# Queries and keys in two float32r parts over 48 rows, with two heads' scores as a pair of row tiles

## The chip, the cores and the metric

The kernel runs on one core of a Trainium2 chip. A core has a matmul engine (TensorE, PE in the profile; its weight loads are listed apart as PEld), VectorE (DVE), ScalarE (ACT), GpSimd (POOL), and queues that issue transfers (SP is the one most used here). They run side by side and wait for each other through semaphores. TensorE writes to eight banks of PSUM, 512 float32 columns each. The metric is the device time of one execution in microseconds, given as the median of several runs. A profile is one further execution with every instruction recorded.

## What is computed

Two rounds of two layers on a residual stream of 2048 tokens by 512. The first layer is full attention with 32 query heads of 16 columns and one common key and value head; the second works in four segments of 512 tokens, with a key and value head for each query head, a mask, and a memory that the segments before have written.

```python
def _A_ref(x, wq, wk, wv, wo):                 # full attention
    q = heads((x @ wq)); k = x @ wk; v = x @ wv
    p = softmax(q @ k.T * 0.25)
    return merge(p @ v) @ wo

def _B_ref(x, wq, wk, wv, wo, beta):           # segment attention with memory
    for s in range(4):
        p = softmax(qs @ ks.T * 0.25 + mask)
        a_mem = (phi(qs) @ M) / (phi(qs) @ z + 1e-6)
        outs.append(g * a_mem + (1 - g) * (p @ vs))
        M += phi(ks).T @ vs;  z += phi(ks).sum()
    return merge(outs) @ wo

x = A_x
x = x + _A_ref(layernorm(x), ...);  x = x + _B_ref(layernorm(x), ...)
x = x + _A_ref(layernorm(x), ...);  x = x + _B_ref(layernorm(x), ...)
```

(Shortened; the names are the reference's, `heads` and `merge` stand for its reshapes.) All of it is float32.

## The kernel before

**Blocks and streams.** Tokens go in four blocks of 512. While the full attention of one block of queries runs (`a_units`), everything that follows from the block before is computed beside it (`side`: output projection, layer norm, segment attention `b_block`, second output projection, and in the first round the inputs of the next full attention, `a_prep`). `weave` (L306) orders the two streams on TensorE while the program is built: it keeps an account of when each engine gets done (`pe`, `on`), and gives the next turn to the stream that lags in proportion to its length. The order is fixed at build time; on the chip TensorE takes its instructions in that order and waits where an operand is late. `finish` (L323) completes a block's full attention alone once the other stream is through.

**Exact products of queries and keys.** A projection's result is split by `split3` (L422) into three bfloat16 parts: one copy on GpSimd (L120) and three operations on VectorE (L428 to L430). The parts go through a scratch in DRAM (`sd`), from which `a_load` and `b_load` lay six groups of 16 rows into the tiles `qa`, `qb` and `kb`; the keys of the full attention are laid out on chip by L444 to L446 into `kst`. Each head's score is one matmul over 96 rows of contraction, and one or two more rows subtract the softmax guard.

**Full attention, a stage.** One stage is one tile of 128 keys for four heads and 512 queries. L600 computes the scores of two heads into two PSUM banks, ScalarE takes the exponential of both at once (L603, 1024 columns), and this is done twice. The products with the values (`a_pv`, L625) are plain float32: four heads go to four column tiles of 17 columns of the array at once. They appear at L77 (the first of a group) and L80 (the other three), since `together` (L74) issues them; a plain float32 matmul shows as two records. There are 1024 stages.

**Segment attention.** `b_inputs` (L710) projects and splits queries and keys and computes their feature maps; `b_rowmax` (L759) computes all scores once for the row maxima, L771, which VectorE takes at L779; `guard_rows` (L546) puts the maxima into rows 96 and 97 of the queries; `b_attend` (L791) computes the scores again with these rows, transposed (L807), adds the mask by a further matmul of 128 columns (L810), and goes on with the exponential (L814) and the values (`b_pv`). Columns that the mask leaves out whole are not computed, so the matmuls have 512, 384, 256 or 128 columns.

**Projections.** `project` (L332) multiplies operands in two float32r parts, three matmuls for each of four contraction tiles (L341), 128 rows and 512 columns each.

## Time and profile before

| | us |
|---|---|
| median of 3 runs | 3379.58 |
| lowest, highest | 3378.01, 3379.90 |
| span of the profiled execution | 3373.7 |
| TensorE busy in it | 3289.8 |
| ScalarE busy in it | 2404.7 |
| VectorE busy in it | 1644.6 |

The span runs from the first to the last instruction; the time of a run holds a little more. Busy time counts an engine as busy from an instruction's start to its end. Matmuls follow each other in a pipeline, so that the length of one is longer than the distance to the next: the distance between starts tells what one costs.

In the lists of costly groups a row names line, engine, operation, tiles and shapes, then the count; behind the first bar the busy time and the mean length of one in ns; behind the second the engine's idle time ahead of them and what ended it. A row of the timeline has start and length in us, then engine, line, operation, tiles, shapes and how many instructions it merges. A row by stretch has start and end, length, busy time of the engines with counts in brackets, the granted TensorE clock, the share of the transfer engines and what they moved in GB/s.

### The profile page before, as it was taken

Reading aid. Unit: us, or ns where it says so; the run is one execution under the profiler, and the core shown is the slowest. Engines: PE = TensorE matmul, PEld = TensorE weight load, DVE = VectorE, ACT = ScalarE, POOL = GpSimd, SP = SyncE. Lnnn points to the kernel's source line nnn. Section 1 sums busy time; section 2 is a strip of 40 time slices with the busy share of each in tenths; the row PEclk is TensorE's granted clock in tenths of the full one; section 3 lists DMA queues with packets and bytes.
Section 4 is the critical chain, followed back from the end, with each engine's and each line's share of the span. In section 5 each row is a group of like instructions: output and inputs, shape, how many; then the busy total and the mean of one; then the engine's idle time right before and its main releaser. Section 6 shows DMA issues by size and latency. Waiting matters only on the chain.

```text
span 3373.7 us, 53649 instructions
## 1 busy us (share of the span) xinstructions
PE 3289.8 (98%) x20586; PEld 1252.0 (37%) x20586; DVE 1644.6 (49%) x4679; ACT 2404.7 (71%) x2575; POOL 377.6 (11%) x540
## 2 busy tenths in 40 slices
PE   7999999999999999999999999999999999999977
PEld 4422333334333443334433333333433334333533
DVE  7701345454553545645455353555455534553466
ACT  3699777866778667786678878677677776778422
POOL 2100110021100220102110020100110002100100
PEclk9999999999999999999999999999999999999978
DMA  4411121122210231202322142321231215221341
GB/s 133 130 33 29 56 84 56 33 78 85 69 54 20 72 91 56 72 15 82 101 64 75 45 123 78 111 61 52 79 85 50 58 39 161 90 65 29 124 121 42
DMA packets 188674, 244.62 MB, mean 73 GB/s; under 512 B 26904, under 2 KB 147576, under 8 KB 188408
## 3 DMA queue, kind: packets, MB, share of 16 engines
q1 hardware_dynamic: 169272, 176.08, 17.7%
q0 software_dynamic: 19136, 65.02, 6.8%
q8 instruction: 164, 2.69, 0.4%
q14 instruction: 102, 0.84, 0.1%
HBM read 168.41 MB, written 72.61 MB: 71 GB/s over the span
## 4 chain that ended last, share of the span: by engine, by line
PE 80%; issue 8%; DVE 5%; DMA 4%; POOL 2%; ACT 1%; SPq 0%; DVEq 0%; POOLq 0%; ACTq 0%
PE bank L77 28%; PE bank L600 24%; PE bank L341 13%; PE bank L771 4%; PE bank L807 4%; PE bank L810 1%; PE bank L80 1%; DMA sb<-parts 1%; PE bank L832 1%; DVE mo L779 1%; DMA wst<-in_B_wq_dram 1%; PE bank L401 1%; POOL w L120 1%; PE bank L868 1%; ACT pa L603 1%
## 5 line engine op out<-in xcount | busy, mean ns | idle before, releaser
L603 ACT ACTIVATE pa<-bank 128x1024 f32<-128x1024 f32 x2048 | 2010.1, 1022 | 610.9 <-PE bank L600 597.2
L600 PE MATMUL bank<-qa,kst 97*128 97x512 bf16 x4096 | 1147.4, 381 | 3.1 <-ACT pa L603 1.8
L80 PE MATMUL bank<-pa,va 128*17 128x512 f32 x6144 | 1072.0, 598 | 0.0
L77 PE MATMUL bank<-pa,va 128*17 128x512 f32 x2048 | 1057.5, 598 | 2.9 <-DVE t L632 1.9
L779 DVE CUSTOM_DVE_ANT_0 mo<-bank,maskq 128x512 bf16<-128x512 f32 (+3 forms) x1024 | 498.7, 487 | 572.7 <-PE bank L771 557.8
L600 PEld LDWEIGHTS <-kst 97*128 97x128 bf16 x4096 | 313.8, 97 | 796.2 <-issue 640.0
L814 ACT ACTIVATE pb<-bank 128x1024 f32<-128x1024 f32 (+2 forms) x384 | 331.6, 881 | 179.8 <-PE bank L810 143.1
L341 PE MATMUL bank<-xh,w 128*128 128x512 f32 x832 | 322.1, 432 | 6.1 <-DVE qmx L471 2.7
L771 PE MATMUL bank<-kb,qb 96*128 96x512 bf16 (+3 forms) x1024 | 251.7, 309 | 26.4 <-DVE m L779 22.9
L341 PE MATMUL bank<-w,xh 128*128 128x512 f32 x752 | 269.8, 437 | 4.7 <-DVE xh L665 2.1
L77 PEld LDWEIGHTS bank<-pa,va 128*17 128x17 f32 x2048 | 117.5, 95 | 406.8 <-issue 325.2
L120 POOL TENSOR_SCALAR w<-wst 128x512 fp32r<-128x512 f32 x160 | 103.8, 649 | 1272.6 <-PE bank L341 1202.0
L807 PE MATMUL bank<-qb,kb 98*128 98x512 bf16 (+3 forms) x1024 | 222.9, 305 | 4.1 <-ACT pb L814 2.8
L632 DVE STREAM_TRANSPOSE t<-bank 128x512 f32<-128x512 f32 x88 | 62.8, 714 | 298.3 <-PE bank L80 297.9
L771 PEld LDWEIGHTS <-qb 96*128 96x128 bf16 x1024 | 87.2, 99 | 302.4 <-issue 247.2
L341 PEld LDWEIGHTS bank<-xh,w 128*128 128x128 f32 x832 | 158.4, 191 | 86.5 <-issue 32.7
L80 PE MATMUL bank<-pb,vb 128*17 128x512 f32 (+3 forms) x1536 | 186.0, 439 | 0.0
L77 PE MATMUL bank<-pb,vb 128*17 128x512 f32 (+3 forms) x512 | 182.6, 439 | 1.0 <-ACT pb L814 0.4
L341 PEld LDWEIGHTS bank<-w,xh 128*128 128x128 f32 x752 | 135.0, 189 | 109.5 <-issue 45.1
L341 PE MATMUL bank<-xl,w 128*128 128x512 f32 x416 | 166.5, 400 | 1.2 <-DVE xl L409 1.2
L208 DVE TENSOR_TENSOR w<-wst,w 128x512 fp32r<-128x512 f32 x160 | 112.0, 700 | 101.0 <-POOL w L120 100.2
L341 PE MATMUL bank<-w,xl 128*128 128x512 f32 x376 | 150.7, 402 | 0.0
(136 smaller groups left out, 2480.5 us busy)
## 6 DMA issues: line engine op xcount, KB each, us to landing
sb<-parts SPq DMA_DIRECT2D x192, 128.0 KB
qa<-sd SPq DMA_DIRECT2D x88, 196.0 KB
sd<-parts SPq DMA_DIRECT2D x96, 128.0 KB
x<-xt SPq DMA_DIRECT2D x48, 256.0 KB
xt<-x SPq DMA_DIRECT2D x48, 256.0 KB
qb<-sb SPq DMA_DIRECT2D x64, 192.0 KB
kb<-sb SPq DMA_DIRECT2D x64, 192.0 KB
qa<-sd SPq DMA_DIRECT2D x88, 128.0 KB
```

Source lines behind the costliest of these rows:

```text
L77: nc.tensor.matmul(*a, **k)
L80: tc.keep_in_program_order(nc.tensor.matmul(*a, **k))
L120: G.tensor_scalar(o, i, 1.0, 0.0, op0=ALU.mult, op1=ALU.add)
L208: V.tensor_tensor(w[:, 1, :], s, f(w[:, 0, :]), op=ALU.subtract)
L341: T.matmul(ps, lhsT=l_(kt), rhs=r_(kt), start=n == 0, stop=n == 11)
L600: T.matmul(sc[:, i, :], lhsT=L["kst"][0:rows, kt * P:(kt + 1) * P], rhs=q[0:rows, 2 * u + i, :], start=True, stop=True)
L603: A.activation(x, sc, AF.Exp, scale=0.25)
L632: V.transpose(t1.rearrange("p a b -> p (a b)"), pva)
L771: T.matmul(ps[:, o_:o_ + nk], lhsT=q[0:96, j, qt * P:(qt + 1) * P], rhs=k[0:96, j, 0:nk], start=True, stop=True)
L779: V.tensor_tensor_reduce(out=mo[:, 0:nk], in0=ps[:, o_:o_ + nk], in1=maskq[:, 512 - nk:512], op0=ALU.add, op1=ALU.max, scale=1.0, scalar=- ...
L807: T.matmul(sc[:, i, o_:o_ + nq], lhsT=k[0:98, 2 * u + i, kt * P:(kt + 1) * P], rhs=q[0:98, 2 * u + i, kt * P:512], start=True, stop=False)
L814: A.activation(e[:, :, 0:w], sc[:, :, 0:w], AF.Exp, scale=0.25)
```

## The change

Queries and keys are split into two float32r parts in place of three bfloat16 parts. Three products (high with high, low with high, high with low) reach the precision, so a head's contraction has 48 rows, and 49 or 50 with the guard. Two heads lie above each other in one tile: one in rows 0 to 63, the other in rows 64 to 127 (`RG = 64`). Their two score matmuls are issued one right after the other, as two row tiles of the array, into two banks.

- `split3` becomes `high` (the copy on GpSimd) and `low` (one subtraction on VectorE, in place of the projection's result). In `b_inputs` the feature map's operations now stand ahead of `low`, and the transposes of the keys' feature map behind the transfers.
- The parts go to DRAM in two transfers of float32 in place of three of bfloat16. A tile of queries or keys comes back in four transfers (two for each half) in place of three.
- The mask of 128 rows is added by two pairs of matmuls over 64 rows each.
- Row maxima stay one matmul for each head and tile of queries; the order of the short ones is changed so that two in one bank come from one half.
- The account gets `DRAIN` for a change between three forms of the array, "full", "rows" and "cols", and other costs for these matmuls. The lengths given to `weave` stay as they are.
- The feature map of the keys and `om` use other tiles, and comments are removed.

```diff
+RG = 64
...
-    def pe(cost):
-        clk["pe"] += cost
+    def pe(cost, form="full"):
+        clk["pe"] += cost + (DRAIN if form != tiling[0] else 0.0)
+        tiling[0] = form
...
-    kst = [st([P, S], BF16, f"kst{i}") for i in range(2)]
+    kst = [st([P, S], F32R, f"kst{i}") for i in range(2)]
-    qa = [st([P, 4, 512], BF16, f"qa{i}") for i in range(2)]
+    qa = [st([P, 2, 512], F32R, f"qa{i}") for i in range(2)]
...
-    def split3(x, t):
-        parts = tmp(2, [P, 3, 512], BF16, "parts")
+    def high(parts, x, t):
         copy_g(parts[:, 0, :], x)
-        t = on("pool", t, 600)
-        r = tmp(2, [P, 512], F32, "rest")
-        V.tensor_tensor(r, x, parts[:, 0, :], op=ALU.subtract)
-        V.tensor_copy(parts[:, 1, :], r)
-        V.tensor_tensor(parts[:, 2, :], r, parts[:, 1, :], op=ALU.subtract)
+        return on("pool", t, 650)
+    def low(parts, x, t):
+        V.tensor_tensor(parts[:, 1, :], x, f(parts[:, 0, :]), op=ALU.subtract)
+        return on("dve", t, 602)
...
+        sd = L["sd"][b].rearrange("(t u i p) r c -> t p i r u c", t=4, u=2, i=2, p=2)[t, p]
+        n_ = 32 if L["exact"] else 33
+        for i in range(2):
+            nc.sync.dma_start(f(q)[RG * i:RG * i + 16], sd[i, 0:16])
+            nc.sync.dma_start(f(q)[RG * i + 16:RG * i + 16 + n_], sd[i, 0:n_])
...
                     for i in range(2):
-                        T.matmul(sc[:, i, :], lhsT=L["kst"][0:rows, kt * P:(kt + 1) * P],
-                                 rhs=q[0:rows, 2 * u + i, :], start=True, stop=True)
+                        r_ = slice(RG * i, RG * i + rows)
+                        together(i == 0, sc[:, i, :], lhsT=L["kst"][r_, kt * P:(kt + 1) * P], rhs=q[r_, u, :],
+                                 start=True, stop=True)
                     x = tmp(4, [P, 2, 512], F32, "pa")
                     A.activation(x, sc, AF.Exp, scale=0.25)
-                    ring.free[k] = on("act", pe(432), 904)
+                    ring.free[k] = on("act", pe(240, "rows"), 904)
...
-        e = pe(940)
+        e = pe(853, "cols")
...
             (w,) = wget("Bq" if which == "q" else "Bk", 1)
             ps, e, rel = yield from project_t(w)
-            qf, t1 = evac(ps, e)
+            parts, qf, t1 = evac(ps, e)
             rel(t1)
-            parts, t2 = split3(qf, t1)
+            t2 = high(parts, qf, t1)
             if (which == "q" and b > 0) or (which == "k" and b < NB - 1):
                 V.tensor_scalar_min(ph, qf, 0.0)
                 A.activation(ph, ph, AF.Exp)
                 V.scalar_tensor_tensor(ph, qf, 0.0, ph, op0=ALU.max, op1=ALU.add)
+            t2 = low(parts, qf, t2)
...
                     for i in range(2):
-                        T.matmul(sc[:, i, o_:o_ + nq], lhsT=k[0:98, 2 * u + i, kt * P:(kt + 1) * P],
-                                 rhs=q[0:98, 2 * u + i, kt * P:512], start=True, stop=False)
-                    for i in range(2):
-                        T.matmul(sc[:, i, o_:o_ + P], lhsT=idb, rhs=maskk, start=False, stop=True)
-                    e_ = pe(2 * cols(nq) + 115)
+                        r_ = slice(RG * i, RG * i + 50)
+                        together(i == 0, sc[:, i, o_:o_ + nq], lhsT=k[r_, u, kt * P:(kt + 1) * P],
+                                 rhs=q[r_, u, kt * P:512], start=True, stop=False)
+                    for a in range(2):
+                        for i in range(2):
+                            r_ = slice(RG * i, RG * i + RG)
+                            together(False, sc[:, i, o_:o_ + P], lhsT=maskk[r_, a, :], rhs=maskk[r_, 2 + a, :],
+                                     start=False, stop=a == 1)
+                    e_ = pe(cols(nq) + 140, "rows")
```

## The prediction

> **What bounds the kernel now.** I read the busy shares first, then the costliest groups, then the busy time by stretch, and last the order of TensorE's matmuls in time.

> ```profile
> span 3373.7 us, 53649 instructions
> PE 3289.8 (98%) x20586; PEld 1252.0 (37%) x20586; DVE 1644.6 (49%) x4679; ACT 2404.7 (71%) x2575; POOL 377.6 (11%) x540
> L603 ACT ACTIVATE pa<-bank 128x1024 f32<-128x1024 f32 x2048 | 2010.1, 1022 | 610.9 <-PE bank L600 597.2
> L600 PE MATMUL bank<-qa,kst 97*128 97x512 bf16 x4096 | 1147.4, 381 | 3.1 <-ACT pa L603 1.8
> ...
> 170.00:372.00 202.00, 202.00 (x1232) 48.78 (x1224) 23.16 (x45) 194.89 (x202) 2.46 (x4) 1.00 0.10 27
> 372.00:2000.00 1628.00, 1616.76 (x10223) 611.83 (x10220) 811.48 (x2310) 1189.87 (x1270) 199.58 (x273) 1.00 0.23 67
> 2000.00:2072.00 72.00, 72.00 (x436) 17.76 (x435) 24.53 (x50) 68.73 (x72) 4.02 (x6) 1.00 0.34 96
> 2072.00:3190.00 1118.00, 1113.02 (x7112) 424.80 (x7111) 541.29 (x1590) 814.29 (x870) 124.27 (x183) 1.00 0.26 76
> 3190.00:3373.00 183.00, 140.73 (x846) 74.24 (x845) 117.28 (x405) 51.01 (x65) 9.99 (x16) 0.86 0.31 92
> ```

> The last five rows are stretches (start:end, length, then busy time of PE, weight loads, VectorE, ScalarE, GpSimd). There are two kinds. In 372–2000 and 2072–3190 full attention is woven with other work: TensorE is full, ScalarE 73% busy. These 2746 us can pay. In 170–372 and 2000–2072 full attention runs alone, and ScalarE is 95 to 96% busy as well. 3190–3373 is the last block by itself; no full attention is left.

> Now the order in time, woven and alone (start, length, instructions):

> ```profile
> 377.72 0.61 PE L600 MATMUL bank<-qa,kst 97*128 97x512 bf16 x2
> 377.97 0.82 PE L341 MATMUL bank<-w,xh 128*128 128x512 f32 x2
> 378.63 0.39 PE L341 MATMUL bank<-w,xl 128*128 128x512 f32 x1
> 378.86 0.61 PE L600 MATMUL bank<-qa,kst 97*128 97x512 bf16 x2
> 379.40 0.60 PE L77 MATMUL bank<-pa,va 128*17 128x512 f32 x1
> 379.40 0.62 PE L80 MATMUL bank<-pa,va 128*17 128x512 f32 x3
> 379.84 0.59 PE L77 MATMUL bank<-pa,va 128*17 128x512 f32 x1
> 379.84 0.61 PE L80 MATMUL bank<-pa,va 128*17 128x512 f32 x3
> 380.38 0.74 PE L341 MATMUL bank<-w,xh 128*128 128x512 f32 x2
> 380.95 0.39 PE L341 MATMUL bank<-w,xl 128*128 128x512 f32 x1
> 381.19 1.04 PE L600 MATMUL bank<-qa,kst 97*128 97x512 bf16 x4
> ...
> 383.30 0.59 PE L77 MATMUL bank<-pa,va 128*17 128x512 f32 x1
> 383.30 0.60 PE L80 MATMUL bank<-pa,va 128*17 128x512 f32 x3
> 383.84 1.04 PE L600 MATMUL bank<-qa,kst 97*128 97x512 bf16 x4
> 384.81 0.60 PE L77 MATMUL bank<-pa,va 128*17 128x512 f32 x1
> ...
> 372.00:2000.00 1628.00, 574.83 (x2036) 156.53 (x2036) 1.00 0.23 67
> 2072.00:3190.00 1118.00, 392.36 (x1379) 104.91 (x1377) 1.00 0.26 76
> ```

> Matmuls overlap, so I use starts, not lengths. A stage (one key tile, four heads) is four scores and eight value matmuls. Four things are to be seen. (1) Four scores take 0.97 us (383.84 to 384.81): 4 x 0.217 and 0.10 for the change to the column tiles of the values. (2) Four column tiles start at once and run beside each other; each round lasts 0.44 (379.40 to 379.84). From the second round to other work passes 0.54: again 0.10 to change the form. (3) A float32r projection matmul behind others takes 0.23 (378.63 to 378.86). (4) Behind a change of form the first float32r matmul takes 0.34 (380.38 to 380.95 is 0.57 for two), 0.11 more: that much of its weight load lies open. The bfloat16 scores in the same place show 0.01 at most (383.84), so a float32r one adds 0.10. Inside one form it does not (377.97 to 378.63 is 0.66 for two, but its first start is recorded while the score before still runs).

> A stage with nothing between thus takes TensorE 0.97 + 0.44 + 0.54 = 1.95 us, and ScalarE 2 x 0.98 = 1.96 (2010.1 us by 2048). Alone, both are bounds at once; woven, only TensorE is.

> **The change part by part**, in the two woven stretches (the last two rows above: 3415 score records, so 1707 pairs).

> *Pairs.* Two scores cost 2 x 0.217 = 0.434. Two row tiles that run together cost at least one matmul, 0.217, and at most two float32r in turn, 0.46. No row shows row tiles; the nearest is the four column tiles that start together. I take one float32r, 0.23. Gain 1707 x 0.205 = **350 us**.

> *Changes of form.* Scores were full-height, like projections and transposes; now they have a form of their own. In the order of the matmul records of the two stretches (the first broken score group after 372 is like 377.72 to 378.86 above; the last is in the next fence), I count 846 entries from values into scores or row maxima, 526 from full-height work into them, and 394 the other way.

> ```profile
> 3161.32 1.04 PE L600 MATMUL bank<-qa,kst 97*128 97x512 bf16 x4
> 3162.01 0.82 PE L341 MATMUL bank<-w,xh 128*128 128x512 f32 x2
> 3162.67 0.40 PE L341 MATMUL bank<-w,xl 128*128 128x512 f32 x1
> ...
> L600 PEld LDWEIGHTS <-kst 97*128 97x128 bf16 x4096 | 313.8, 97 | 796.2 <-issue 640.0
> L341 PEld LDWEIGHTS bank<-xh,w 128*128 128x128 f32 x832 | 158.4, 191 | 86.5 <-issue 32.7
> ```

> From values the 0.10 is paid already; new is the open float32r load: 846 x 0.10 = **85 us**. From full-height work both are new: 526 x (0.10 + 0.09) = **100 us**. Back to it likewise, less where a transpose follows: 394 x 0.18 = **71 us**. The bounds: nothing, if such a change needs no pause and loads stay hidden; or another 0.11 for the second row tile's load if the two loads go one behind the other. I take the middle, one open load, since the four column tiles show no such steps.

> [...]

> *Segment attention.* 896 masked score matmuls of 512, 384, 256 and 128 columns become 448 pairs; 896 row maxima stay single.

> ```profile
> 489.58 0.59 PE L807 MATMUL bank<-qb,kb 98*128 98x512 bf16 x2
> 490.01 0.28 PE L810 MATMUL bank<-maskk,idb 128*128 128x128 bf16 x2
> ...
> 490.65 0.50 PE L807 MATMUL bank<-qb,kb 98*128 98x384 bf16 x2
> 490.99 0.28 PE L810 MATMUL bank<-maskk,idb 128*128 128x128 bf16 x2
> 491.11 0.38 PE L771 MATMUL bank<-kb,qb 96*128 96x512 bf16 x1
> ```

> They take 0.217, 0.17, and by width 0.11 and 0.056: 0.55 for the four. In float32r none comes under its 0.11 load: 0.23 + 0.175 + 0.12 + 0.11 = 0.635. Scores gain 112 x (1.09 - 0.635) = **51 us**; row maxima lose 224 x 0.09 = **20 us**. Masks go from two of 0.06 to two pairs of 0.06: nothing. The short float32r widths are shown nowhere; at the rate of the values (plain float32: two rounds of 0.44, four times a score) 128 columns would be 0.22, 40 us more in all; at bfloat16's rate 25 us less.

> *Other work.* VectorE loses two of the three operations that split queries and keys (0.44 and 0.69 us each time), but the low part now lies behind the feature map and overwrites what ScalarE reads, so it can wait an exponential (1.0 us) with row maxima queued behind it. In the woven stretches VectorE is under half busy and TensorE's other stream covers this. Without cover it is some 2 us for each of the last block's eight inputs, against 1.1 saved, and half of them have no feature map; I put that block at 5 us gained, and the 60 or so woven stages before 170 at 8 (0.12 a stage, the sum below over 853 stages). The loads of queries grow from three to four transfers of nearly equal bytes (97 x 4 x 1 KB against 98 x 2 x 2 KB); the scores' idle time of 3.1 us in all (L600 above) says that they are early.

> ```profile
> L429 DVE CAST parts<-rest 128x512 bf16<-128x512 f32 x104 | 45.4, 436 | 1.4
> L430 DVE TENSOR_TENSOR parts<-rest,parts 128x512 bf16<-128x512 f32 x104 | 72.2, 695 | 1.4
> ```

> *What does not gain.* In 170–372 and 2000–2072 ScalarE's 1.96 stays: nothing. About 70 stages of the woven stretches also stand alone, like 383.84 to 384.81; their share of the gain, 70 x 0.31, is taken off: **22 us**.

> **Sum**: 350 + 51 - 85 - 100 - 71 - 20 - 22 = 103 us, and 13 outside: 116. Span 3258. The shown median, 3379.58, lies 5.9 us above the span, which I keep: **3264 us**. Next late is TensorE still, with ScalarE at some 76%.

> **The rivals.**

> *A, loads and changes cost less.* If the open loads hide behind the 0.10 pause, the three terms shrink from 256 to (526 + 394) x 0.10 = 92; 164 us more gain, less some 15 for ScalarE at over 80%: **3115**. For it: the scores now carry half the matmul time. Against: row (4) shows an open load.

> *B, slower: the two row tiles' loads go one behind the other.* Place: the first pair behind each change of form, 1116 entries (522 + 409 by full attention, 185 by segment attention). Price 0.11 each, 123 us, and 28 in the short pairs, which then take 0.22 at least: the gain of 116 becomes -35, **3415**. It decides once over 0.084 us of the second load lies open. For it: one matmul follows its own load. Against: the four loads of the column tiles cost no visible step. [...]

> *C, float32r row tiles do not run together at all.* Pairs then cost 0.46: 41 us lost for 350 gained, 20 lost for 51, and stages that stand alone pass ScalarE's 1.96: about **3730**. This is also the case in which the change doesn't do what it says. Against: the column tiles, float32 too, do run together.

> *D, ScalarE takes over.* The planned order counts 0.904 us per exponential where it takes 0.98; if pieces of two or three stages become bound by it, the gain halves: **3320**.

> **How the numbers follow.** The forecast 0.47 (its own range 3215 to 3315), A 0.25, B 0.18, C 0.05, D 0.05. The range 3100 to 3420 holds the forecast, D, most of A and most of B, and the bounds of the short widths; it leaves out C and the ends of A and B. Faster by over 0.2% (7 us, about what a measurement of this kernel can tell from no change): forecast, A, D: 0.77. Within: a forecast short by its whole gain or B short by half, 0.05. Slower: B and C, 0.18.

> **What would show it.** Two scores of a pair starting within 0.02 us, the next pair 0.23 later (pairs; 0.46 would be C). From the second value round to the second pair 0.54 + 0.33 (one open load; 0.23 would be A, 0.44 B). From a pair to a projection 0.33 instead of 0.23. Stretches of full attention alone unchanged at 1.96 a stage. ScalarE some 76% busy while woven, VectorE's two splitting operations gone. The forecast is wrong if the new order breaks score groups much more often than 0.6 times a stage: each further break costs about 0.37 us, so 300 more would take all of the gain.

## The result, and the profile after

| | us |
|---|---|
| predicted | 3264 (3100 to 3420) |
| after, median of 4 runs | 3504.68 (3483.66 to 3524.46) |
| before, median of 4 runs | 3378.80 |
| ratio after to before, with its 95% interval | 1.0371 [1.0330, 1.0412] |
| span of the profiled execution after | 3504.2 |

The kernel became slower by 126 us, where a gain of 116 was forecast. The four runs after lie 41 us apart, in the order of their granted clock (3483.66 us at 0.967, 3524.46 at 0.953); the profiled one, 3506.11, is near their median. The page of the kernel after, in the order of its parts (span and busy shares, granted clock in 40 slices, the chain that ended last, costly groups):

```profile
span 3504.2 us, 55847 instructions
PE 3306.5 (94%) x21610; PEld 1374.9 (39%) x21610; DVE 1541.7 (44%) x4454; ACT 2382.0 (68%) x2575; POOL 375.7 (11%) x541
...
PEclk8999999999999999998999989999999999989867
...
PE 63%; issue 14%; ACT 10%; DVE 6%; DMA 4%; POOL 2%; SPq 0%; ACTq 0%; POOLq 0%; DVEq 0%
...
L619 ACT ACTIVATE pa<-bank 128x1024 f32<-128x1024 f32 x2048 | 1992.3, 1030 | 596.5 <-PE bank L87 583.3
...
L84 PE MATMUL bank<-qa,kst 49*128 49x512 f32 x2048 | 899.9, 474 | 26.7 <-ACT pa L619 14.3
L87 PE MATMUL bank<-qa,kst 49*128 49x512 f32 x2048 | 894.0, 473 | 0.0
...
L84 PEld LDWEIGHTS bank<-qa,kst 49*128 49x128 f32 x2048 | 356.7, 186 | 734.5 <-ACT pa L619 324.8
```

Score pairs are L84 and L87 now (the two halves), the exponential is L619. Four things have changed. TensorE is busy for 17 us more but for 94% of the span, not 98%: it now has idle time. The granted clock dips within the run too, and further at its end. And the weight loads of the scores, whose idle time "issue" ended before, are held up by ScalarE (324.8 of 734.5 us). The chain of the kernel before, for comparison, had ScalarE at 1%, where it has 10% now:

```profile
PE 80%; issue 8%; DVE 5%; DMA 4%; POOL 2%; ACT 1%; SPq 0%; DVEq 0%; POOLq 0%; ACTq 0%
```

The matmuls in time, in a stage of full attention alone and in a woven stretch of the kernel after (start, length, instructions):

```profile
252.18 0.60 PE L84 MATMUL bank<-pa,va 128*17 128x512 f32 x1
252.19 0.62 PE L87 MATMUL bank<-pa,va 128*17 128x512 f32 x3
252.62 0.59 PE L84 MATMUL bank<-pa,va 128*17 128x512 f32 x1
252.63 0.61 PE L87 MATMUL bank<-pa,va 128*17 128x512 f32 x3
253.16 0.49 PE L84 MATMUL bank<-qa,kst 49*128 49x512 f32 x1
253.17 0.49 PE L87 MATMUL bank<-qa,kst 49*128 49x512 f32 x1
253.50 0.39 PE L84 MATMUL bank<-qa,kst 49*128 49x512 f32 x1
253.50 0.39 PE L87 MATMUL bank<-qa,kst 49*128 49x512 f32 x1
254.01 0.60 PE L84 MATMUL bank<-pa,va 128*17 128x512 f32 x1
...
603.89 0.49 PE L84 MATMUL bank<-qa,kst 49*128 49x512 f32 x1
603.89 0.49 PE L87 MATMUL bank<-qa,kst 49*128 49x512 f32 x1
604.31 0.50 PE L352 MATMUL bank<-xh,w 128*128 128x512 f32 x1
604.65 0.39 PE L352 MATMUL bank<-xl,w 128*128 128x512 f32 x1
604.88 0.40 PE L352 MATMUL bank<-xh,w 128*128 128x512 f32 x1
605.21 0.49 PE L84 MATMUL bank<-qa,kst 49*128 49x512 f32 x1
```

The prices stand as forecast. The halves of a pair start together; from the second value round to the first pair it is 0.54 us, to the second pair 0.34 more (0.23 and one open load). A pair between values and a projection takes 0.42 (603.89 to 604.31; by the forecast's prices 0.23, 0.10 for its load, 0.09 for the change). Rivals B and C are refuted: the two loads of a pair go together (those of the second pair start at 253.27 and 253.28 and take 0.19 each). So the loss must come from order and waiting. Stretches of both kernels show where (start:end, length, busy time of PE, weight loads, VectorE, ScalarE, GpSimd, then the granted clock); first before, then after:

```profile
1500.00:1570.00 70.00, 70.00 (x429) 26.86 (x427) 29.73 (x77) 50.40 (x54) 7.92 (x12) 1.00 0.18 55
1570.00:1610.00 40.00, 38.87 (x205) 18.00 (x204) 23.35 (x38) 22.48 (x26) 12.52 (x16) 1.00 0.29 84
3168.00:3374.00 206.00, 162.03 (x942) 90.10 (x934) 136.68 (x460) 52.67 (x68) 14.34 (x24) 0.87 0.36 111
```

```profile
1500.00:1570.00 70.00, 69.09 (x554) 27.01 (x555) 25.50 (x80) 59.01 (x64) 1.25 (x2) 1.00 0.06 16
1570.00:1610.00 40.00, 25.75 (x93) 15.85 (x91) 22.81 (x58) 3.59 (x4) 7.78 (x11) 0.73 0.29 85
2000.00:2072.00 72.00, 56.56 (x258) 27.34 (x248) 36.27 (x85) 24.62 (x27) 12.81 (x18) 0.83 0.34 100
3209.00:3504.00 295.00, 239.00 (x1323) 132.41 (x1315) 152.76 (x510) 63.48 (x82) 15.67 (x26) 0.76 0.27 84
```

In 1500–1570 the kernel after runs more exponentials (64 against 54) and hardly any work for GpSimd; in 1570–1610 ScalarE is all but idle: the block's full attention has run out, and the other stream goes on alone, with TensorE 64% busy and the clock down to 0.73. In 2000–2072, where full attention ran alone before, the other stream is alone for more than half of it (no score starts for 39.5 us from 2000.5 on). The last stretch of each starts where the last full attention ends: 206 us were left before, 295 are left now.

For an account I took the distance from each matmul's start to the next, by the kind of the first (what a distance has over 0.65 us counts as a wait, and all distances under a halved clock go by themselves). "Woven" runs from the end of the 128th stage (356 us before, 357 after) to the last full attention; `share84` and `hybrid_proj12` are experiments below. Us, worked out from the traces:

| | before | forecast | after | share84 | hybrid_proj12 |
|---|---|---|---|---|---|
| scores of full attention | 836 | −210 | −86 | −76 | −99 |
| full-height work | 615 | +83 | +16 | +30 | −15 |
| scores of segment attention | 124 | −32 | −20 | −14 | 0 |
| row maxima | 132 | +50 | −21 | −22 | +40 |
| masks | 67 | +6 | +22 | +31 | +5 |
| products with values | 1031 | 0 | −23 | −5 | −4 |
| waits | 8 | 0 | +42 | +15 | +16 |
| at half clock | 0 | 0 | +111 | +17 | +14 |
| woven, sum | 2812 | −103 | +40 | −24 | −42 |
| from there to the last matmul | 198 | −5 | +89 | +58 | +9 |

The forecast's terms stand where their distance falls. The scores of full attention have 22 − 350, the open loads of their 522 + 409 entries (93) and the pause behind them in 277 of the 394 changes back (25). The loads of the other 441 entries and the other 117 pauses are added to segment attention's own terms: 19 to its scores, 30 to the row maxima, 6 to the masks. Full-height work has 47 + 35.

### The profile page after: what moved, and what is told of

Its sections match the earlier page's. It is cut to its first block, busy times and chain, and to the rows that moved or that the text cites. A ratio compares the mean times of both kernels' runs of the same rounds, so it can differ in the third digit from the quotient of the medians.

```text
span 3504.2 us, 55847 instructions
## 1 busy us (share of the span) xinstructions
PE 3306.5 (94%) x21610; PEld 1374.9 (39%) x21610; DVE 1541.7 (44%) x4454; ACT 2382.0 (68%) x2575; POOL 375.7 (11%) x541
## 4 chain that ended last, share of the span: by engine, by line
PE 63%; issue 14%; ACT 10%; DVE 6%; DMA 4%; POOL 2%; SPq 0%; ACTq 0%; POOLq 0%; DVEq 0%
PE bank L84 37%; PE bank L352 14%; ACT pa L619 9%; PE bank L87 4%; PE bank L790 4%; DVE mo L798 1%; PE bank L856 1%; ACT pb L838 1%; POOL w L130 1%; PE bank L412 1%; DMA sb<-parts 1%; PE bank L892 1%; POOL parts L130 1%; DMA wst<-in_B_wk_dram 1%; DVE w L219 1%
## 5 line engine op out<-in xcount | busy, mean ns | idle before, releaser
L619 ACT ACTIVATE pa<-bank 128x1024 f32<-128x1024 f32 x2048 | 1992.3, 1030 | 596.5 <-PE bank L87 583.3
L87 PE MATMUL bank<-pa,va 128*17 128x512 f32 x6144 | 1086.6, 605 | 0.0
L84 PE MATMUL bank<-pa,va 128*17 128x512 f32 x2048 | 1070.7, 605 | 15.9 <-DVE t L648 4.0
L84 PE MATMUL bank<-qa,kst 49*128 49x512 f32 x2048 | 899.9, 474 | 26.7 <-ACT pa L619 14.3
L87 PE MATMUL bank<-qa,kst 49*128 49x512 f32 x2048 | 894.0, 473 | 0.0
L84 PEld LDWEIGHTS bank<-qa,kst 49*128 49x128 f32 x2048 | 356.7, 186 | 734.5 <-ACT pa L619 324.8
L352 PE MATMUL bank<-xh,w 128*128 128x512 f32 x832 | 346.9, 449 | 13.3 <-DVE t L858 5.0
L87 PEld LDWEIGHTS bank<-qa,kst 49*128 49x128 f32 x2048 | 356.1, 186 | 1.4 <-DMA qa<-sd 0.8
L790 PE MATMUL bank<-kb,qb 48*128 48x128 f32 (+3 forms) x1024 | 316.1, 374 | 37.1 <-DVE m L798 28.3
L790 PEld LDWEIGHTS bank<-kb,qb 48*128 48x128 f32 x1024 | 177.5, 198 | 332.5 <-DVE m L798 163.2
L84 PEld LDWEIGHTS bank<-pa,va 128*17 128x17 f32 x2048 | 116.7, 95 | 314.5 <-issue 233.9
L84 PE MATMUL bank<-qb,kb 50*128 50x512 f32 (+3 forms) x512 | 202.7, 414 | 4.1 <-ACT pa L619 1.9
L87 PE MATMUL bank<-qb,kb 50*128 50x512 f32 (+3 forms) x512 | 205.2, 415 | 0.0
L87 PE MATMUL bank<-pb,vb 128*17 128x512 f32 (+3 forms) x1536 | 196.7, 461 | 0.0
L84 PE MATMUL bank<-pb,vb 128*17 128x512 f32 (+3 forms) x512 | 193.4, 461 | 1.5 <-ACT pb L838 1.3
```

What stands on the lines that cost most here:

```text
L84: nc.tensor.matmul(*a, **k)
L87: tc.keep_in_program_order(nc.tensor.matmul(*a, **k))
L352: T.matmul(ps, lhsT=l_(kt), rhs=r_(kt), start=n == 0, stop=n == 11)
L619: A.activation(x, sc, AF.Exp, scale=0.25)
L790: T.matmul(ps[:, o_:o_ + nk], lhsT=q[r_, u, qt * P:(qt + 1) * P], rhs=k[r_, u, 0:nk], start=True, stop=True)
```

## Experiments

The expectations weigh several theories. Three stood at the start. **W**: the lengths given to `weave` are those of the old kernel. Full attention's stages are shorter in the new account, but its length is still 1814 ns a stage, so it gets too many turns and runs out early. **P**: changes of form and open loads cost more than forecast. **C** (not the prediction's rival C): the chain of the other stream's own work became longer. Two came up later. **G**: in the last block shorter matmuls leave TensorE idle enough to lose half its clock. **S**: pairs come faster than ScalarE frees the PSUM slots of scores.

**The stale lengths, from both sides.** `TAF` (L41) multiplies full attention's length in `weave` (L1024). `share84` is the changed kernel with

```diff
-TAF = 1.0
+TAF = 0.84
```

> The changed kernel with one number edited: the length of a full-attention stage that the weave is told of goes from 1814 to 1524 (its own price in the account). Theory W (the weave gives full attention too large a share, so that it runs out and the side work is left alone, on a half-idle TensorE at half clock): the 332 matmuls more that stand behind the last full-attention matmul go, the time falls by 60 to 120 us, to 3385-3445. Theory P (the matmul prices are worse than forecast: changes of form and open weight loads): the number of changes of form is nearly the same (3555 against 3591), so 3480-3520. Theory C (the chain of the side work itself became longer): the same, 3470-3520.

Measured: 3424.37 us, ratio to before 1.0143 [1.0118, 1.0168]; 80 of the 126 us lost are back, as W expected and neither P nor C. The profiled run (3409.32) is the lowest of its four, 15 us under their median. The stretch of `share84` that had run dry, and the first woven stretch as a whole:

```profile
1570.00:1610.00 40.00, 38.52 (x211) 18.81 (x203) 19.60 (x29) 23.25 (x26) 14.94 (x19) 1.00 0.35 104
372.00:2000.00 1628.00, 1595.11 (x10802) 659.95 (x10801) 761.15 (x2201) 1193.42 (x1282) 195.72 (x270) 1.00 0.24 71
```

Now the kernel before, with the error put in:

```diff
-TAF = 1.0
+TAF = 1.19
```

> The kernel before with the opposite edit alone: the stage length that the weave is told of is 19% too large (2159 in place of 1814), as it is in the changed kernel. Theory W: full attention runs out early here too, 129 matmuls more stand behind it, and the kernel before loses 30 to 70 us: 3410-3450. Theories P and C: nothing, 3375-3385.

Measured: 3454.75 us, 1.0218 [1.0201, 1.0235], 76 us lost, a little more than expected. The same stretch of this kernel:

```profile
1500.00:1570.00 70.00, 69.96 (x501) 24.43 (x500) 25.53 (x81) 57.63 (x62) 1.32 (x2) 1.00 0.04 13
1570.00:1610.00 40.00, 30.15 (x143) 14.69 (x141) 18.84 (x52) 12.07 (x12) 5.09 (x9) 0.83 0.24 79
```

It is the picture of after (62 exponentials, then 12) with not one score matmul changed. W is shown from both sides: some 80 us, mostly as half clock and waits and as a longer last block.

**Fewer changes of form.** In `share84` a projection is issued whole (its three turns between contraction tiles go), or the two pairs of a stage come as one block, once two slots are free (`both()`):

```diff
 # share84_proj12, in project()
-            if kt < 3:
-                yield lambda: 0.0
 # share84_blocks, in a_units()
-                    yield lambda: max(need, rings["sc"].ready(), L["kr"][kt // 4], gate(f, n, k1))
+                    if u == 0:
+                        yield lambda: max(need, rings["sc"].both(), L["kr"][kt // 4], gate(f, n, k1))
```

> The edit of share84, and a projection's twelve matmuls are no longer cut into four pieces between which full attention may come: 310 changes of form less (3245 against 3555), nearly all of them between full-height work and row tiles. By the prices that the trace of the changed kernel shows (0.10 for the change and 0.11 open load each way) 50 to 65 us less than share84. Theory W alone: no better than share84, rather worse by 0 to 20, since ScalarE waits up to 2.7 us.

> The edit of share84, and the two score pairs of a stage are given to TensorE as one block (once both score slots are free): 158 fewer changes from row tiles to full height, 131 fewer in all. By the prices 20 to 30 us less than share84; against it the exponentials of a stage must both be done before the next scores start: if ScalarE becomes the bound the time rises by 50 us or more over share84.

Measured: 3395.57 (1.0050 [1.0034, 1.0065]) and 3395.93 (1.0045 [1.0028, 1.0062]), 29 and 28 us under `share84`. In the built order the changes of form go from 3555 to 3245 and to 3424: 0.09 us for each one saved in the first case, 0.21 in the second. Whole projections were expected to give 50 to 65 us; they gave half of it. Both together:

> Both orders together (whole projections, both score pairs of a stage in one block): 370 changes of form fewer than share84, 60 to 80 us by the prices; alone each gave 29. If they add up: 3355-3375, below the kernel before. If the freed time turns into waits and half clock: 3385-3400.

Measured: 3399.24, 1.0071 [1.0052, 1.0090], with 3185 changes. The two gains don't add up: that longer blocks of one form also make the other stream wait would explain it, but was not measured. That projections in one piece are no gain of their own shows in the kernel before with the same edit as `share84_proj12`:

> The kernel before with whole projections (twelve matmuls in one piece) and nothing else. In it scores and projections have one form, so nothing is saved by not cutting them. If share84_proj12 gained its 29 us by the changes of form and the open loads: no gain here, 3375-3395. If whole projections are better for another reason (order, waits): 3345-3365.

Measured: 3390.89, 1.0034 [1.0022, 1.0047], 13 us slower. What the edit saves in `share84` is thus put down to the new forms, by elimination; it is no fixed price for each change, as the two orders together show. The number of changes hardly grew: 3529 in the order before, if scores are counted as a form of their own there too, 3591 after, 3555 in `share84`. The named failure (score groups broken more often) did not happen.

**The last block.** In `share84` it takes 263 us at a clock of 0.74, against 206 at 0.87 before. If half clock came from idle time (G), more work for TensorE should end it. `share84_tail_doubled` issues, in the last block alone, each row maximum's matmul three times and each score pair twice:

```diff
-                T.matmul(ps[:, o_:o_ + nk], lhsT=q[r_, u, qt * P:(qt + 1) * P], rhs=k[r_, u, 0:nk],
-                         start=True, stop=True)
+                for _ in range(3 if tail[0] else 1):
+                    T.matmul(ps[:, o_:o_ + nk], lhsT=q[r_, u, qt * P:(qt + 1) * P], rhs=k[r_, u, 0:nk],
+                             start=True, stop=True)
...
+                    for d in range(2 if tail[0] else 1):
...
```

> The kernel of share84; in the last block alone, which runs without full attention, each row-maximum matmul is issued three times and each score pair twice into the same place (some 50 us of TensorE work more at full clock, which computes nothing new). Theory G (the clock gate: paired and shorter, the matmuls leave TensorE too little to do in the last block, it is put to half clock for 107 us of 256 in place of 36 of 198, and what it then does takes twice as long): the half clock shrinks, and the last block takes 256 or less in spite of the added work; the time 3390-3425. Rival (the last block is longer because its chain of transfers and VectorE work is longer, and the half clock only follows): the added work comes on top, 3435-3475.

Measured: 3440.62, 1.0176 [1.0159, 1.0193]: slower by 16 than `share84`, and the clock stayed down. G as stated falls; the time lies where the rival, a longer chain with the half clock only following, was expected. The successor of G, **R**, supposes that the granted clock follows how many rows of the array are in use, so that matmuls of 48 to 50 rows count for less than those of 128. `share84_tail_full_filler` adds, in the last block, two full-height matmuls ahead of each group of row maxima:

```diff
+            for _ in range(2 if tail[0] else 0):
+                T.matmul(ps, lhsT=bnk, rhs=maskq, start=True, stop=True)
...
```

> The kernel of share84; in the last block alone two matmuls of 128 rows and 512 columns that compute nothing go into the same place ahead of each group of row maxima (160 in all, 35 us at full clock, and some 50 changes of form each way). Doubling the half-height matmuls there left the half clock at 125 us with TensorE seemingly busy. Theory R (what keeps the clock up is rows in use and not time in use: 48 or 50 rows count as less than half): the half clock of the last block falls from 107 to under 60 us, and the time is 3395-3430 in spite of the added work. Rival (the clock follows something else, such as the gaps between the instructions): the half clock stays above 100 and the time is 3435-3475.

Measured: 3420.95, 1.0134 [1.0117, 1.0151]: no slower than `share84` for all the added work, and the last block is 240 us to the last matmul, against 256. The last stretches of `share84`, of the doubled and of the filled kernel, one fence each:

```profile
3144.00:3407.00 263.00, 212.72 (x1099) 120.22 (x1095) 135.32 (x446) 52.80 (x68) 14.49 (x24) 0.74 0.31 95
```

```profile
3166.00:3449.00 283.00, 256.10 (x1487) 174.60 (x1480) 134.65 (x447) 53.52 (x68) 14.49 (x24) 0.75 0.29 89
```

```profile
3157.00:3406.00 249.00, 217.56 (x1248) 113.77 (x1255) 132.83 (x447) 52.18 (x68) 14.36 (x24) 0.92 0.33 101
```

TensorE busy for 256 of 283 us is granted 0.75, busy for 218 of 249 it is granted 0.92. Time at half clock, added up from the trace's clock records behind the last full attention: 130, 133 and 31 us (48 before; the expectations leave waits out of theirs and have 107, 125 and, before, 36). Busy time at half clock is itself stretched (in the kernel after, a round of value products takes 0.83 us there, 3359.20 to 3360.03, against 0.44 at full clock, 252.18 to 252.62), so stretches at full clock compare better. First the doubled kernel, which falls to half clock behind one of 95%, then the filled kernel, which stays at full clock at 93%:

```profile
3346.50:3380.50 34.00, 32.28 (x273) 21.35 (x270) 23.89 (x78) 11.60 (x15) 1.55 (x2) 1.00 0.29 80
3380.50:3418.00 37.50, 37.50 (x235) 24.08 (x233) 16.56 (x67) 7.73 (x9) 0.00 (x0) 0.50 0.01 3
```

```profile
3259.00:3398.70 139.70, 130.29 (x915) 61.20 (x920) 85.70 (x305) 39.29 (x48) 2.68 (x4) 1.00 0.19 56
```

The unprofiled runs agree: over the whole kernel the four of `share84` were granted 0.965 to 0.975, those of the doubled kernel 0.967 to 0.974, those of the filled one 0.977 to 0.985. The longest idle gap of TensorE there does not separate these runs: it is 6.2, 4.8 and 5.7 us. What separates them is the added work: thin matmuls did not raise the clock, full-height ones did. The fillers are bfloat16 as well, where the thin matmuls are float32r; but in 3144–3200 of `share84`, where all matmuls are full-height float32, TensorE is granted 1.00 at 86% busy (48.24 of 56 us), so the type alone does not explain it. R fits all of this. Whether the clock follows rows, cells or something else that goes with them is open.

**Full attention in pairs, segment attention as before.** `hybrid` is `share84` with the segment attention's three bfloat16 parts, 98 rows and full-height masks put back:

```diff
-    qb = [st([P, 2, 512], F32R, f"qb{i}") for i in range(3)]
-    kb = [st([P, 2, 512], F32R, f"kb{i}") for i in range(3)]
+    qb = [st([P, 4, 512], BF16, f"qb{i}") for i in range(3)]
+    kb = [st([P, 4, 512], BF16, f"kb{i}") for i in range(3)]
...
```

> The kernel of share84 with segment attention as in the kernel before (three bfloat16 parts, one score after the other, full height, masks by one matmul of 128 rows); only full attention keeps the row pairs. The last block should take 198 us again in place of 256 (theories G and the longer chain alike). While woven, 896 masks cost 67 in place of 98 us, but segment scores and row maxima now stand at full height between the row tiles: 341 changes of form more, 35 to 70 us. Together 3365-3425. If the last block stays at 250, the two-part split isn't what lengthens it.

Measured: 3376.10, 0.9992 [0.9983, 1.0002], 48 us under `share84` and level with before. Its last stretch:

```profile
3150.00:3375.00 225.00, 171.37 (x986) 97.09 (x980) 141.80 (x472) 52.99 (x69) 15.04 (x25) 0.88 0.34 107
```

The clock is back at 0.88 with 44 us at half. From the last full attention to the last matmul it is 214 us, against 256 in `share84`; these 42 are more than the whole difference of the two profiled runs (3407.0 and 3375.7). `hybrid` puts several things back at once, the height, the split and the transfers. The transfers are no larger part of the chain in `share84`: writes of the parts (`sb<-parts`) make up 8.4% of the chain that ended last in 3168–3374 before, 4.7% in 3144–3407 of `share84`. The other suspect of the last block was the chain through VectorE, with the low part behind the feature map. `share84_low_first` puts it, and the transfers, ahead again:

```diff
-        x = f(parts)[:, 1, :]
+        x = tmp(1, [P, 512], F32, "qf")
...
-            t2 = high(parts, qf, t1)
+            t2 = low(parts, qf, high(parts, qf, t1))
+            sd = dram.tile([8, 32, 512], F32, tag=f"sb{which}{t % 2}", name=nm("sb"))
+            for c in range(2):
+                nc.sync.dma_start(sd[:, 16 * c:16 * c + 16, :], f(parts[:, c, :]))
```

> The kernel of share84 with the low part and its transfers ahead of the feature map, as in the order of the kernel before (the projection's result lies in a tile of its own for it). If the moved subtraction, which waits for ScalarE's exponential, lengthens the side chain (theory C): 10 to 30 us less, 3395-3415, most of it in the last block. If it is covered: 3415-3435.

Measured: 3412.34, 1.0102 [1.0085, 1.0118]. The four runs lie within the spread of `share84` (3409.32 to 3436.32), so the 12 us are hardly clear of noise. The time is in the range given for C, but the gain is not in the last block, which takes 265 us (256 in `share84`). That order is not what makes it long.

**A version that beats both.** `hybrid` with whole projections:

> The kernel of hybrid with whole projections: 106 changes of form less. By the prices 20 to 30 us less than hybrid: 3345-3360, below the kernel before. If the longer pieces starve ScalarE instead: 3370-3390.

Measured: 3347.64 us, 0.9912 [0.9896, 0.9929], 31 us under before, with 28 us for 106 changes of form fewer than `hybrid`. With stages in blocks besides:

> The kernel of hybrid with whole projections and with both score pairs of a stage in one block: 487 changes of form less than hybrid (3409 against 3896), and the second pair of each block finds its loads hidden. By the prices 80 to 110 us less than hybrid, 3270-3300; with the waits for ScalarE that blocks showed in share84_blocks_proj12, half of it: 3320-3340.

Measured: 3347.85, 0.9907 [0.9891, 0.9924]: nothing more for a further 381 changes of form, where even the cautious expectation had 3320 to 3340. So the number of changes does not forecast what an order gains.

**Why pairs give less than 350.** Even in `share84` the scores take 134 us more than forecast. A pair that stands second and is followed by values should take 0.33; its mean in the woven stretches is 0.40. The waits of weight loads in 372–2000 (what they waited for: us, times, longest), before and in `share84`:

```profile
PEld L600 <- issue: 298.2, 547, 0.9
```

```profile
PEld bank L84 <- issue: 255.4, 795, 1.4
PEld bank L84 <- ACT pa L619: 224.5, 381, 1.3
```

Line L84 holds other loads too. Of the 381, 333 are loads for full attention's scores (tile `kst`: us, times), and the other 48 are for segment attention's:

```profile
  ACT pa L619: 194.4, 333
```

Before, none of the scores' loads waits for ScalarE, and their matmuls do so twice, for 0.4 us. The 194.4 us are idle time ahead of weight loads and not time that TensorE lost: its matmuls stood idle for 7.2 us on this account. What a wait costs shows in the pairs. Of 357 second pairs ahead of values whose halves start together, 165 take 0.33 us or little more, and no load of theirs waited for ScalarE; 191 take about 0.42, and in 162 of these a load did. Two experiments take this apart. `share84_bf16_scores` reads the operands of full attention's scores as the upper halves of the same words, bfloat16, in the same order of instructions:

```diff
+    def top(ap):
+        return ap.bitcast(BF16).rearrange("p (c t) -> p c t", t=2)[:, :, 1]
-                        together(i == 0, sc[:, i, :], lhsT=L["kst"][r_, kt * P:(kt + 1) * P], rhs=q[r_, u, :],
-                                 start=True, stop=True)
+                        together(i == 0, sc[:, i, :], lhsT=top(L["kst"])[r_, kt * P:(kt + 1) * P],
+                                 rhs=top(q[:, u, :])[r_, :], start=True, stop=True)
```

> The kernel of share84 in the same order, instruction for instruction; the score pairs of the full attention read the upper halves of their float32r operands as bfloat16 (every second 16-bit word), so the scores are less exact, and only the type of these 4096 matmuls and of their weight loads differs. In share84 a pair costs 0.434 us on the mean of the woven stretches (forecast 0.34 with all its changes of form), and 0.33 behind a row maximum where 0.23 was forecast. If open float32r loads are what the pairs lost: behind a change of form and behind a row maximum a pair falls from 0.33 to 0.24, some 1400 pairs by 0.10, 80 to 140 us less: 3285-3345. If the pairs wait for something else (the form's pause, the score slots, ScalarE): less than 30 us, 3395-3425.

Measured: 3340.88, 0.9884 [0.9865, 0.9904], 84 us under `share84`. A first pair behind projections falls from 0.34 to 0.24, the second ahead of values from 0.40 to 0.35 on the mean. No load of these scores waits for ScalarE here; the wait stands on their matmuls and is short (tile `kst`; the exponential is L622):

```profile
  ACT pa L622: 13.3, 62
```

In the account of the profiled runs, against `share84`, the scores lose 125 us and the woven part 63: row maxima (32), half clock (17) and waits (12) take the rest back.

`share84_half_exp` leaves ScalarE half its work in full attention. It takes the exponential of 256 of the 512 columns, and the products with the values read these twice:

```diff
-                    A.activation(x, sc, AF.Exp, scale=0.25)
+                    A.activation(x[:, :, 0:256], sc[:, :, 0:256], AF.Exp, scale=0.25)
...
+                     rhs=x[j // 2][:, j % 2, 0:256].unsqueeze(1).broadcast_to([P, 2, 256]),
```

> The kernel of share84, but the full attention's exponentials are taken of half the columns (256 of 512), and the value matmuls read these columns twice; the rest of the probabilities is left out. ScalarE's work per stage falls by some 0.8 us, TensorE's stays; the order comes out with 145 changes of form less (25 us), and the stretch of full attention alone is no longer held by ScalarE (20 us). Theory S (while woven, pairs wait for score slots that ScalarE has not emptied: 381 weight loads of scores wait for its exponentials in 372-2000, none did before): 50 to 90 us more, in all 3285-3335. If ScalarE does not hold the woven stretches: 45 us in all, 3370-3390.

Measured: 3322.35, 0.9835 [0.9800, 0.9869], 102 us under `share84`. By the account of the profiled runs 20 us lie ahead of the 128th stage, where ScalarE is the bound (in `share84` its exponentials take 178.13 of 187 us in 170–357), and 75 in the woven part, 71 of them in the scores, whose second pair takes 0.33 here too. Second pairs at 0.42 are nearly gone, 14 against 259 at 0.33. Some 13 to 15 of the 75 are fewer changes of form (145 at 0.09 to 0.10). So **S** is real; its size, some 60 us, is an estimate from one run whose order differs too. The loads' waits for ScalarE (tile `kst`) fell little beside it, which again makes them no measure of what is lost:

```profile
  ACT pa L619: 163.8, 229
```

S and the loads are not separate sums: 162 of the 191 second pairs at about 0.42 us are pairs whose float32r load had waited for ScalarE.

Lone row maxima add to it. The row tiles of `share84` in time:

```profile
641.57 0.49 PE L84 MATMUL bank<-qa,kst 49*128 49x512 f32 x1
641.57 0.49 PE L87 MATMUL bank<-qa,kst 49*128 49x512 f32 x1
641.91 0.40 PE L790 MATMUL bank<-kb,qb 48*128 48x512 f32 x1
641.94 0.50 PE L87 MATMUL bank<-qa,kst 49*128 49x512 f32 x1
642.14 0.40 PE L84 MATMUL bank<-qa,kst 49*128 49x512 f32 x1
```

The row maximum L790 uses one half only, so one score of the next pair (L87) starts beside it and the other (L84) 0.20 later. The pair is split, and the row maximum hardly takes time of its own: in some 200 places behind values the next score starts 0.01 us after it on the median. That is why row maxima got cheaper and not dearer, 132 to 110 us in `share84`, and part of why the scores did not. The two are best read together: −98 us where −160 were forecast.

## Why the prediction was wrong, point by point

- **A pair at 0.23, halves together: right** (253.50 for both). So were the open load (0.34 from pair to pair), the 0.54 from values, and the 0.42 of a pair between values and a projection. The forecast's choice of one open load, not two, is borne out (0.34, where two would give 0.44).
- **The three terms for changes of form, 256 us: their part in loads right in size.** Open loads ahead of full attention's scores, 0.10 for each of 522 + 409 entries, were forecast at 93 us; bfloat16 operands in the same order gave 84, though that holds loads behind a wait too. The number of changes held as well (3529 to 3555). The pauses are not priced as well: fewer changes gave from 0.27 us each to nothing. The named sign of failure, score groups broken more often, did not come.
- **The step that failed first is the one that took the stretches of before as given.** The gain was worked out "in the two woven stretches", as if the same work lay beside the same work afterwards. The order is planned with lengths that the diff leaves alone, and they no longer fitted. It cost 80 us. None of the rivals named it, though the code of `weave` and the diff were enough to see it.
- **"I put that block at 5 us gained": wrong in sign.** To the last matmul it takes 58 us more even in `share84`. With its thin matmuls it is at half clock for 130 us, against 48 before; `hybrid` gives 48 us for putting segment attention back as it was. The forecast looked at VectorE's chain alone there and put the clock at nothing, though the row of before, 0.86 in 3190–3373, showed that this block did not hold its clock even then.
- **350 us for pairs: mis-sized as a whole.** The pair's own price held, but the scores gained 76 where 210 were due, and scores and row maxima together 98 where 160 were due. The missing step is the ring of score slots: a stage's scores took 0.97 us before, about one exponential (0.98), and ScalarE could free a slot meanwhile. Rival D has this engine, but as a bound on whole stretches; it came as short waits inside stages, with ScalarE 73% busy over the stretch (1193.42 of 1628 us in `share84`; 76% were forecast).
- **Segment attention, with its changes of form: scores −14 in place of −32, masks +31 in place of +6, row maxima −22 in place of +50.** Full-height work took 30 more in place of 83. Against the forecast that is 25 us dearer for the masks and 18 for the scores, 72 cheaper for the row maxima, which run beside halves of score pairs, and 53 for full-height work: together 82 cheaper. The forecast's prices by width, none under 0.11, were estimates: in the kernel after, a pair behind masks took 0.31 us with 512 columns, 0.20 with 256 and 0.15 with 128 (3213.86, 3484.41 and 3486.15, each to its mask), where 0.23, 0.12 and 0.11 were put.
- **Alone 1.96 unchanged: wrong, and it gave nothing.** A stage takes 1.83 (252.18 to 254.01): the starts of ScalarE's exponentials lie 0.91 apart there. But the 128th stage ended at 357 us, as before at 356. The start had lost what this gained: the 32nd stage ended at 176.1 us, before at 167.9, where 8 us less were forecast for the start, and the granted clock in 45–170 was 0.94, before 0.99. Why it was lower there was not followed up.
- **VectorE, transfers: right.** VectorE's busy time fell from 1644.6 to 1541.7 us, and the loads of queries (`qa<-sd`) hold up the scores' weight loads for no more than 0.8 us in the rows of the page.

In all, the profiled run missed the forecast span of 3258 by 246 us: 143 in the woven part (−103 forecast, +40 found), 94 in the last block, 9 at the start and end. With the lengths mended (`share84`, span 3407.0) 149 are left: 79, 63 and 7. The 79 are 134 for the scores, 15 for waits and 17 at half clock, less the 82 above and 5 for products with values. Not tried: more PSUM slots for scores (the eight banks of the kernel's tile `bank` are all taken), lengths fitted anew for `hybrid`, and row maxima in pairs.

## What to carry to other kernels

When a change makes one of two interleaved streams cheaper, look first for the numbers that share out the turns: a correct price with a stale share lost 80 us here, and 0.84 in one line gave them back. What the packing of short matmuls gave here was held down by the consumer of the results (some 60 of the 102 us that half of ScalarE's exponentials gave, an estimate) and by the operand's weight load (84 us less with bfloat16 scores, waits among them): full attention kept its pairs with a profit once projections were whole (31 us under before), segment attention was better left as it was, at full height (48 us). Ahead of a forecast, look up each stretch whose granted clock is already under 1.00: here the last block went from 0.87 to 0.74 with thinner matmuls (`share84`) and took 58 us more.
